# Turning z: TensorE transposes and ScalarE copies, or VectorE block transposes and SBUF-to-SBUF DMAs, with a new written order

## The chip, the cores and the metric

The kernel runs on one core of one Trainium2 chip. The metric is the device time of one execution in microseconds (us). Each time given for a kernel is a median of several runs; a profile is a record of one single execution. The engines of the core are TensorE (PE in the profile, with its weight loads as PEld), VectorE (DVE), ScalarE (ACT), GpSimd (POOL) and SyncE (SP), whose instruction queue issues most of the DMAs here.

## The reference

Two blocks follow each other. The first is a gated linear recurrence over 768 steps for 4 batches and 8 heads of width 48: a complex decay, its size held to at most 0.999, multiplies a 48x48 state, and k v is added to it; q reads it out. The second is a feed-forward block on all 3072 rows of 384 values:

```python
h = x @ w_in                       # 384 -> 1024
e = np.exp(h - h_max)
sm = e / (np.sum(e, axis=-1, keepdims=True) + 1e-09)
solu = h * sm
ln = (solu - mu) / np.sqrt(var + 1e-06) * g_ln
return (ln @ w_out).astype(np.float32)   # 1024 -> 384
```

All is float32. The kernel before and the changed one compute the same.

## The kernel before

The fast path (`whole`) cuts the 3072 rows into 24 chunks of 128 rows: chunk c has time tile c // 4 of batch c % 4. Two chunks make a group g, for which q, k, v and the two parts of the decay are loaded and prepared together (logarithms, an angle, running sums by a triangular matmul). For each chunk the prepared q and k are turned by TensorE (`f_turned`), scores are computed and masked (`f_score`, `f_att`), values and the state are multiplied in (`f_y`), and the state is carried on (`f_d`, `f_state`). Then comes the feed-forward block of that chunk (`ffn_steps`): `turn_x` and `turned_x` bring x into the layout with features on partitions; `up` multiplies by w_in into two halves of 512 columns (`f_h`, line 961); `exp` and `solu` make z, 128 rows by 1024 features (`f_z`); z is turned in two halves by four TensorE transposes each into PSUM (`f_zt`, line 981), and each half is copied to SBUF by ScalarE (`f_zT`, line 984). `down` multiplies the eight 128-row blocks of zT by w_out in two halves (`f_o`, line 1008). `norm` takes mean and variance of z by VectorE and GpSimd, `scale` multiplies the result by 1/sigma with ScalarE, `store` writes 128x384 values to DRAM.

The weights come in a wide form and are converted at the start (`fetch`, `raised`, `convert`); `again` and `inspect` load each piece of them once more later and look at its smallest value, for the check (`verdict`) that chooses between the fast path and the general one.

The order of work is written out by hand as text. Each word such as `zt0:-1` names a step and a chunk. START is gone through once; then, for n from 2 to 25, EVEN for even n and ODD for odd n, with chunk n plus the number behind the colon (`g1` means group n // 2 + 1). A step is carried out where it is first named. A step issues its instructions on the engines in this order, and each engine, SP's queue of DMAs among them, goes through its own instructions strictly in the order written, waiting where data or a buffer isn't ready. So one pair of turns, EVEN and ODD, does two chunks and one group.

Buffers that matter: `f_z` and `f_zT` have two each, `f_o` one bank of PSUM, `f_h` two banks, the PSUM pool `f_ps_t`, which all turns share, two. DMAs on SP are the loads (line 626), `load_vr` (line 637: the odd heads of v with their four 32-row blocks in reverse, eight DMAs of 32 partitions for a group), the weight pieces (line 657), the small rows `f_ends` (line 767) and `f_on` (line 826), and the stores (line 1018).

Of the kernel before, what the change touches and what calls it, by code (L numbers as in the profile page):

```python
# [11 lines left out]
FP = mybir.dt.float32  # L12
# [7 lines left out]
P = 128  # L20
# [490 lines left out]


START = """
load_ar:0 load_ai:0 fetch:0 fetch:1 fetch:4 fetch:3 clamp:0 inverse:0 fetch:2 ratio:0 raised:0 load_ar:1
tangent:0 raised:1 square:0 convert:1 secant:0 load_q:0 size:0 fourth:0 eps:0 fetch:5 convert:0 raised:4 lnm:0
load_ai:1 convert:4 total0:0 raised:2 total1:0 low0:0 raised:3 low1:0 decay:0 convert:3 qs1:0 grow:0 trig:0
angle:0 raised:5 fetch:6 qs0:0 phase0:0 convert:2 phase1:0 nearest0:0 nearest1:0 clamp:1 ends:0 part0:0 part1:0
load_k:0 raised:6 fetch:12 convert:5 ks0:0 cos:0 turn_ends:0 sin:0 exp:0 load_v:0 ks1:0 k2:0 kt1:0 tot:0 kt0:0
inverse:1 q2:0 kT1:0 gain:0 qt1:0 kT0:0 qt0:0 load_vr:0 fetch:8 q2:1 k2:1 qT1:0 convert:6 qT0:0 ratio:1 kt0:1
fetch:10 raised:12 score0:0 kt1:1 kT0:1 score1:0 qt1:1 mask0:0 fetch:9 fetch:7 fetch:11 kT1:1 load_vr:1 qt0:1  # L520
mask1:0 raised:8 qT1:1 values:0 tangent:1 score1:1 load_k:1 raised:9 mean:0 x:0 qT0:1 turn_x:0 square:1 load_q:1
convert:12 turned_x:0 secant:1 convert:8 carry:0 score0:1 size:1 raised:7 fetch:13 mask1:1 convert:7 up0:0 eps:1
raised:11 trig:1 lnm:1 angle:1 load_q:2 convert:9 raised:10 mean:1 add:0 total1:1 total0:1 mean:2 low1:1
phase0:1 low0:1 mask0:1 nearest0:1 raised:13 phase1:1 load_ar:2 convert:11 nearest1:1 fourth:1 mean:3 load_v:2
load_q:4 part0:1 part1:1 cos:1 values:1 convert:10 sin:1 x:1 convert:13 up1:0 exp:1 decay:1 qs0:1 mean:4 grow:1
mean:5 turn_x:1 q2:2 mean:6 exp0:0 mean:7 qt0:2 ks0:1 turned_x:1 k2:2 solu0:0 carry:1 centre:5 centre:2 kt0:2
kT0:2 qT0:2 up0:1 centre:7 load_ai:2 zt0:0 score0:2 centre:4 centre:3 centre:0 centre:1 exp1:0 centre:6 zT0:0
kt1:2
"""
EVEN = """  # L530
turn_x:-1 solu1:-2 score0:0 zt1:-2 down0:-2 clamp:g1 load_k:g1 inverse:g1 turned_x:-1 kt1:0 ks1:g0 zT1:-2 add:-1
again:-8 qs1:g0 kT1:0 qt1:0 ratio:g1 up0:-1 tangent:g1 q2:1 load_vr:g0 up1:-1 load_v:g0 qT1:0 square:g1 qt0:1
secant:g1 qt1:1 exp0:-1 qT0:1 k2:1 mask0:0 size:g1 score1:0 qT1:1 kt1:1 down1:-2 kt0:1 exp1:-1 norm:-2 ends:g0
kT1:1 eps:g1 kT0:1 solu1:-1 solu0:-1 mask1:0 lnm:g1 values:0 trig:g1 turn_ends:g0 tot:g0 x:0 total0:g1 low0:g1
angle:g1 scale:-2 total1:g1 score0:1 low1:g1 store:-2 zt0:-1 zT0:-1 on:g1 zt1:-1 mask0:1 score1:1 phase0:g1
zT1:-1 phase1:g1 nearest0:g1 mask1:1 carry:0 down0:-1 part0:g1 add:0 nearest1:g1 load_ai:g2 fourth:g1 part1:g1
cos:g1 again:-3 inspect:-7 turn_x:0 values:1 turned_x:0 x:1 sin:g1 up0:0 load_q:g2 up1:0 exp:g1 grow:g1 ks0:g1
k2:2 decay:g1 kt0:2 qs0:g1 exp0:0 solu0:0 q2:2 norm:-1 zt0:0 carry:1 kT0:2
"""
ODD = """  # L540
inspect:-9 qt0:1 qT0:1 zT0:-1 down1:-2 load_ar:g2 exp1:-1 scale:-2 store:-2
"""


# [8 lines left out]
def whole(ctx, tc, flag, q, k, v, a_re, a_im, moe_w_in, moe_w_out, moe_g_ln, out):  # L553
# [12 lines left out]
    nc = tc.nc  # L566
# [3 lines left out]
    FF = moe_w_in.shape[1]  # L570
# [5 lines left out]
    def pool(name, bufs, **kw):  # L576
        return ctx.enter_context(tc.tile_pool(name=name, bufs=bufs, **kw))
# [13 lines left out]
    ident, tri, _, turns, ones = (mats[:, i] for i in range(5))  # L591
# [354 lines left out]
    def ffn_steps(n):  # L946
        st = {}

        def turn_x():
            ps = st["xt"] = ps_t.tile([P, DM], FP, tag="t", padded_shape=[P, 512], name="f_xt")  # L950
            for c in range(KD):
                nc.tensor.transpose(out=ps[:, c * P:(c + 1) * P], in_=T["x", n][:, c * P:(c + 1) * P], identity=ident)  # L952

        def turned_x():
            st["xT"] = ffp.tile([P, DM], FP, tag="xT", name="f_xT")
            nc.scalar.copy(out=st["xT"], in_=st["xt"])

        def up(half):
            h = ps_h.tile([P, 512], FP, tag="h", name="f_h")
            for c in range(KD):  # L960
                nc.tensor.matmul(out=h, lhsT=st["xT"][:, c * P:(c + 1) * P],  # L961
                                 rhs=w_in[:, c, half * 512:(half + 1) * 512], start=(c == 0), stop=(c == KD - 1))
            st["h", half] = h

        def exp(half):
            if half == 0:
                st["z"] = ffp.tile([P, FF], FP, tag="z", name="f_z")
            nc.scalar.activation(out=st["z"][:, half * 512:(half + 1) * 512], in_=st["h", half], func=AF.Exp,  # L968
                                 accum_out=sums[:, n, half:half + 1])

        def solu(half):
            z = st["z"][:, half * 512:(half + 1) * 512]
            nc.vector.tensor_tensor(out=z, in0=st["h", half], in1=z, op=OP.mult)  # L973

        def turn_z(half):
            if half == 0:
                st["zT"] = zp.tile([P, FF], FP, tag="zT", name="f_zT")
            ps = st["zt", half] = ps_t.tile([P, 512], FP, tag="t", name="f_zt")
            for i in range(4):
                c = half * 4 + i  # L980
                nc.tensor.transpose(out=ps[:, i * P:(i + 1) * P], in_=st["z"][:, c * P:(c + 1) * P], identity=ident)  # L981

        def turned_z(half):
            nc.scalar.copy(out=st["zT"][:, half * 512:(half + 1) * 512], in_=st["zt", half])  # L984

        def norm():

            z = st["z"]  # L990
            bs = sml.tile([P, FF // 512, 6], FP, tag="bs", name="f_bs")
            mv = sml.tile([P, 2], FP, tag="mv", name="f_mv")
            s2 = sml.tile([P, 1], FP, tag="s2", name="f_s2")
            st["rs"] = sml.tile([P, 1], FP, tag="rs", name="f_rs")
            for i in range(FF // 512):
                nc.vector.bn_stats(out=bs[:, i], in_=z[:, i * 512:(i + 1) * 512])  # L996
            nc.vector.bn_aggr(out=mv, in_=bs)
            se = sml.tile([P, 1], FP, tag="se", name="f_se")
            nc.vector.tensor_tensor(out=se, in0=sums[:, n, 0:1], in1=sums[:, n, 1:2], op=OP.add)
            nc.vector.scalar_tensor_tensor(out=s2, in0=se, scalar=1e-6, in1=se, op0=OP.mult, op1=OP.mult)  # L1000
            nc.gpsimd.tensor_tensor(out=s2, in0=s2, in1=mv[:, 1:2], op=OP.add)
            nc.gpsimd.tensor_tensor(out=st["rs"], in0=s2, in1=mhalf, op=OP.pow)

        def down(half):
            if half == 0:
                st["o"] = ps_o.tile([P, DM], FP, tag="o", padded_shape=[P, 512], name="f_o")
            for c in range(half * KF // 2, (half + 1) * KF // 2):
                nc.tensor.matmul(out=st["o"], lhsT=st["zT"][:, c * P:(c + 1) * P], rhs=w_out[:, c],  # L1008
                                 start=(c == 0), stop=(c == KF - 1))

        def scale():
            st["out"] = ffp.tile([P, DM], FP, tag="ot", name="f_ot")
            nc.scalar.activation(out=st["out"], in_=st["o"], func=AF.Copy, scale=st["rs"])

        def store():
            ti, b = divmod(n, B)
            r0 = b * S + ti * P
            nc.sync.dma_start(out=out[r0:r0 + P, :], in_=st["out"])

        own = dict(turn_x=turn_x, turned_x=turned_x, norm=norm, scale=scale, store=store)  # L1020
        for half in range(2):
# [123 lines left out]
```

## Time and profile before

| | |
|---|---|
| median of 3 runs | 506.89 us (505.1 to 508.81) |
| profiled execution, its own time | 505.1 us |
| span of the profiled execution | 503.3 us |
| granted TensorE clock | 0.996 |
| DMA queue of SP and its share of 16 engines | 147856 packets, 43.34 MB, 38.8% |
| ScalarE copies f_zT | 48, mean 587 ns, 26.9 us |
| TensorE transposes f_zt | 192, mean 279 ns, 28.0 us |

How to read the profile: busy time is the time in which an engine has at least one instruction under way. Matmuls of TensorE overlap in the pipeline, so the mean duration of one is longer than what it costs; the distance from one start to the next is closer to that. The chain of waits is followed back from the last instruction, at each step to what released it. A window is a stretch of the span in us from its start; a timeline merges instructions of the same line that follow each other, with start, duration and count (weight loads are counted together with their matmuls, so x8 are four transposes). For a DMA, the issue is the time for which SP is held, and "to landing" the time from the issue until the data are there.

### The profile page before, as it was taken

What the parts mean: (1) busy time and instruction counts of PE and PEld (TensorE: products, weight loads), DVE (VectorE), ACT (ScalarE), POOL (GpSimd) and SP (SyncE); (2) the same over time, 40 slices, a digit from 0 to 9 for tenths busy, and PEclk for the clock granted to TensorE, in tenths of its full rate; (3) what the DMA queues carried; (4) which work ended last, traced back from release to release, by engine and by line L of the source; (5) the groups of instructions that cost most, each with busy time, mean ns of one, the idle gap of its engine ahead of it and who ended that gap; (6) DMA issues with size and microseconds to landing.
All of it is one profiled execution on the core that took longest, in us unless ns stands there. A gap on an engine that the chain in (4) does not pass through costs nothing.

```text
span 503.3 us, 15535 instructions
## 1 busy us (share of the span) xinstructions
PE 463.2 (92%) x6756; PEld 294.1 (58%) x6756; DVE 358.3 (71%) x692; ACT 314.9 (63%) x521; POOL 18.0 (4%) x52
## 2 busy tenths in 40 slices
PE   0258998999999999999999999999999999999994
PEld 0036456567566566566666666666666666667552
DVE  5899999586677687687687687687687687672331
ACT  4989948666667667657657657657657657734120
POOL 0000000000000000000000000000000000010000
PEclk9999999999999999999999999999999999999998
DMA  9867950331332542452452451452452342021001
GB/s 232 202 138 211 187 96 23 77 79 33 84 78 50 118 119 54 114 123 53 102 131 46 104 122 38 112 119 41 113 117 43 81 114 48 17 48 34 3 16 39
DMA packets 148079, 44.76 MB, mean 89 GB/s; under 512 B 141217, under 2 KB 144289, under 8 KB 148001
## 3 DMA queue, kind: packets, MB, share of 16 engines
q1 hardware_dynamic: 147856, 43.34, 38.8%
q8 instruction: 55, 0.90, 0.8%
q10 hardware_dynamic: 144, 0.33, 0.2%
q14 instruction: 24, 0.19, 0.1%
HBM read 38.87 MB, written 4.72 MB: 87 GB/s over the span
## 4 chain that ended last, share of the span: by engine, by line
PE 83%; DVE 7%; ACT 4%; DMA 2%; SPq 2%; issue 1%; ACTq 0%
PE f_o L1008 24%; PE f_h L961 23%; PE f_turned L864 8%; PE f_score L895 6%; PE f_zt L981 4%; PE f_phase L805 4%; PE f_L L754 4%; PE f_y L913 4%; PE f_d L929 3%; PE f_y L916 3%; SPq L626 2%; PE f_xt L952 1%; DMA f_raw<-in_moe_w_in_dram 1%; DMA f_v<-in_v_dram 1%; DVE f_k L854 1%
## 5 line engine op out<-in xcount | busy, mean ns | idle before, releaser
L1008 PE MATMUL f_o<-f_w_out,f_zT 128*128 128x384 f32 x384 | 132.9, 489 | 0.4 <-ACT f_zT L984 0.4
L961 PE MATMUL f_h<-f_w_in,f_xT 128*128 128x512 f32 x288 | 129.3, 597 | 0.0
L1008 PEld LDWEIGHTS f_o<-f_w_out,f_zT 128*128 128x128 f32 x384 | 69.4, 190 | 40.7 <-ACT f_zT L984 0.6
L961 PEld LDWEIGHTS f_h<-f_w_in,f_xT 128*128 128x128 f32 x288 | 52.7, 190 | 57.7 <-issue 56.4
L973 DVE TENSOR_TENSOR f_z<-f_h,f_z 128x512 f32<-128x512 f32 x48 | 32.0, 686 | 39.6 <-ACT f_z L968 39.6
L868 ACT COPY f_kT<-f_turned 96x512 f32<-96x512 f32 x48 | 27.8, 581 | 48.7 <-PE f_turned L864 48.1
L868 ACT COPY f_qT<-f_turned 96x512 f32<-96x512 f32 x48 | 26.8, 582 | 30.6 <-PE f_turned L864 30.6
L984 ACT COPY f_zT<-f_zt 128x512 f32<-128x512 f32 x48 | 26.9, 587 | 18.4 <-PE f_zt L981 18.4
L968 ACT ACTIVATE f_z<-f_h 128x512 f32<-128x512 f32 x48 | 28.6, 596 | 14.3 <-PE f_h L961 14.3
L754 PE MATMUL f_L<-f_lr,f_mats 128*128 128x384 f32 x48 | 19.9, 540 | 19.1 <-DVE f_lr L749 18.8
L895 PEld LDWEIGHTS f_score<-f_qT,f_kT 96*32 96x32 f32 x1536 | 30.6, 110 | 11.7 <-issue 11.3
L895 PE MATMUL f_score<-f_qT,f_kT 96*32 96x128 f32 (+3 forms) x1536 | 37.1, 236 | 0.0
L899 DVE TENSOR_TENSOR f_att<-f_score,f_mats 128x512 f32<-128x512 f32 x48 | 32.7, 682 | 5.8 <-PE f_score L895 5.8
L921 DVE COPY f_xn<-f_y 128x384 f32<-128x384 f32 x24 | 13.2, 552 | 30.9 <-PE f_y L916 28.4
L864 PE MATMUL f_turned<-f_mats,f_k 128*96 128x128 f32 x192 | 30.4, 283 | 5.1 <-DVE f_k L854 4.8
L864 PEld LDWEIGHTS f_turned<-f_mats,f_k 128*96 128x96 f32 x192 | 22.1, 130 | 18.9 <-issue 7.4
L996 DVE BATCH_NORM_STATS2 f_bs<-f_z 128x6 f32<-128x512 f32 x48 | 30.7, 681 | 0.0
L916 PE MATMUL f_y<-f_state,f_qT 96*32 96x48 f32 x1280 | 30.1, 205 | 0.0
L864 PE MATMUL f_turned<-f_mats,f_q 128*96 128x128 f32 x192 | 28.1, 282 | 1.9 <-ACT f_ar L732 0.8
L981 PE MATMUL f_zt<-f_mats,f_z 128*128 128x128 f32 x192 | 28.0, 279 | 0.3 <-DVE f_z L973 0.3
L916 PEld LDWEIGHTS f_y<-f_state,f_qT 96*32 96x32 f32 x1280 | 27.7, 110 | 0.0
L864 PEld LDWEIGHTS f_turned<-f_mats,f_q 128*96 128x96 f32 x192 | 21.2, 129 | 10.5 <-issue 5.4
(101 smaller groups left out, 732.7 us busy)
## 6 DMA issues: line engine op xcount, KB each, us to landing
f_raw<-in_moe_w_in_dram SPq DMA_DIRECT2D x12, 512.0 KB, 5.8
f_raw<-in_moe_w_out_dram SPq DMA_DIRECT2D x16, 384.0 KB, 4.6
f_ar<-in_a_re_dram SPq DMA_DIRECT2D x24, 192.0 KB, 3.4
f_ai<-in_a_im_dram SPq DMA_DIRECT2D x24, 192.0 KB, 4.0
f_q<-in_q_dram SPq DMA_DIRECT2D x24, 192.0 KB, 3.8
f_k<-in_k_dram SPq DMA_DIRECT2D x24, 192.0 KB, 3.7
f_v<-in_v_dram SPq DMA_DIRECT2D x24, 192.0 KB, 3.4
out_dram<-f_ot SPq DMA_DIRECT2D x24, 192.0 KB, 2.0
```

The lines of the kernel that those rows point to most:

```text
L754: nc.tensor.matmul(out=ps, lhsT=tri, rhs=st["lr"][:, i * DM:(i + 1) * DM], start=True, stop=True)
L864: nc.tensor.transpose(out=ps[0:D2, j], in_=T[nm + "2", c][:, half * 4 + j].rearrange("p u d -> p (u d)"), identity=ident)
L868: nc.scalar.copy(out=T[nm + "T", c][:, half * 512:half * 512 + 512], in_=st[nm, half][0:D2].rearrange("p i t -> p (i t)"))
L895: nc.tensor.matmul(out=ps[r0:r0 + 32, i, r:], lhsT=KT[:, x * P + r:x * P + r + 32], rhs=QT[:, x * P + r:(x + 1) * P], start=True, stop=True)
L899: nc.vector.tensor_tensor(out=st["att"][:, half * 4:half * 4 + 4].rearrange("p (i u) t -> p i u t", u=2), in0=scores[half].rearrange("p (i ...
L916: nc.tensor.matmul(out=y[r:r + 32, hs], lhsT=T["qT", c][:, x * P + r:x * P + r + 32], rhs=state[b][:, hs], start=False, stop=True)
L961: nc.tensor.matmul(out=h, lhsT=st["xT"][:, c * P:(c + 1) * P], rhs=w_in[:, c, half * 512:(half + 1) * 512], start=(c == 0), stop=(c == KD ...
L968: nc.scalar.activation(out=st["z"][:, half * 512:(half + 1) * 512], in_=st["h", half], func=AF.Exp, accum_out=sums[:, n, half:half + 1])
L973: nc.vector.tensor_tensor(out=z, in0=st["h", half], in1=z, op=OP.mult)
L981: nc.tensor.transpose(out=ps[:, i * P:(i + 1) * P], in_=st["z"][:, c * P:(c + 1) * P], identity=ident)
L996: nc.vector.bn_stats(out=bs[:, i], in_=z[:, i * 512:(i + 1) * 512])
L1008: nc.tensor.matmul(out=st["o"], lhsT=st["zT"][:, c * P:(c + 1) * P], rhs=w_out[:, c], start=(c == 0), stop=(c == KF - 1))
```

## The change

The steps `zt0`, `zt1` (TensorE) and `zT0`, `zT1` (ScalarE) fall away. In their place stand two steps for each chunk. `blocks` has VectorE transpose the whole z, 128x1024, in blocks of 32x32 into a new buffer `f_zb`, of which there is one. Each block then lies turned in its old place. `turn_z` moves the blocks to their places with 16 DMAs from SBUF to SBUF on SP's queue: for each pair of 32-partition bands r and s, one DMA takes from band r the 32 columns at s of each of the eight 128-column groups, and writes them to band s at the columns r. So each of the 16 DMAs moves 32 partitions x 8 pieces x 128 bytes, 32 KB. `down` then reads `f_zT` as before, but each of its matmuls needs all four bands. `scale` is still done by ScalarE with the same instruction; only its place in the order is new.

The three texts START, EVEN and ODD are replaced as a whole, so that every step of every engine, and every DMA, has a new place. The number of all other steps is unchanged.

```diff
--- before.py
+++ after.py
@@ -511,34 +511,34 @@
 
 
 START = """
-load_ar:0 load_ai:0 fetch:0 fetch:1 fetch:4 fetch:3 clamp:0 inverse:0 fetch:2 ratio:0 raised:0 load_ar:1
-tangent:0 raised:1 square:0 convert:1 secant:0 load_q:0 size:0 fourth:0 eps:0 fetch:5 convert:0 raised:4 lnm:0
-load_ai:1 convert:4 total0:0 raised:2 total1:0 low0:0 raised:3 low1:0 decay:0 convert:3 qs1:0 grow:0 trig:0
-angle:0 raised:5 fetch:6 qs0:0 phase0:0 convert:2 phase1:0 nearest0:0 nearest1:0 clamp:1 ends:0 part0:0 part1:0
-load_k:0 raised:6 fetch:12 convert:5 ks0:0 cos:0 turn_ends:0 sin:0 exp:0 load_v:0 ks1:0 k2:0 kt1:0 tot:0 kt0:0
-inverse:1 q2:0 kT1:0 gain:0 qt1:0 kT0:0 qt0:0 load_vr:0 fetch:8 q2:1 k2:1 qT1:0 convert:6 qT0:0 ratio:1 kt0:1
-fetch:10 raised:12 score0:0 kt1:1 kT0:1 score1:0 qt1:1 mask0:0 fetch:9 fetch:7 fetch:11 kT1:1 load_vr:1 qt0:1
-mask1:0 raised:8 qT1:1 values:0 tangent:1 score1:1 load_k:1 raised:9 mean:0 x:0 qT0:1 turn_x:0 square:1 load_q:1
-convert:12 turned_x:0 secant:1 convert:8 carry:0 score0:1 size:1 raised:7 fetch:13 mask1:1 convert:7 up0:0 eps:1
-raised:11 trig:1 lnm:1 angle:1 load_q:2 convert:9 raised:10 mean:1 add:0 total1:1 total0:1 mean:2 low1:1
-phase0:1 low0:1 mask0:1 nearest0:1 raised:13 phase1:1 load_ar:2 convert:11 nearest1:1 fourth:1 mean:3 load_v:2
-load_q:4 part0:1 part1:1 cos:1 values:1 convert:10 sin:1 x:1 convert:13 up1:0 exp:1 decay:1 qs0:1 mean:4 grow:1
-mean:5 turn_x:1 q2:2 mean:6 exp0:0 mean:7 qt0:2 ks0:1 turned_x:1 k2:2 solu0:0 carry:1 centre:5 centre:2 kt0:2
-kT0:2 qT0:2 up0:1 centre:7 load_ai:2 zt0:0 score0:2 centre:4 centre:3 centre:0 centre:1 exp1:0 centre:6 zT0:0
-kt1:2
+load_ar:0 load_ai:0 fetch:0 fetch:2 clamp:0 fetch:1 inverse:0 ratio:0 load_ar:1 fetch:6 tangent:0 raised:0
+raised:2 convert:0 fetch:4 fetch:5 square:0 secant:0 size:0 fourth:0 eps:0 load_k:0 raised:6 gain:0 convert:2
+lnm:0 total1:0 convert:6 low1:0 raised:1 fetch:3 load_q:0 total0:0 raised:4 load_ai:1 low0:0 fetch:7 decay:0
+convert:4 grow:0 trig:0 angle:0 phase0:0 raised:5 nearest0:0 phase1:0 convert:1 ks0:0 nearest1:0 fetch:9 ks1:0
+mean:0 fetch:10 convert:5 part0:0 part1:0 raised:3 cos:0 qs1:0 qs0:0 sin:0 clamp:1 q2:0 load_k:1 k2:0 k2:1 qt0:0
+exp:0 inverse:1 qT0:0 kt0:0 kt0:1 kT0:0 kT0:1 qt1:0 ratio:1 load_vr:0 score0:0 qT1:0 q2:1 tangent:1 kt1:0
+raised:7 kT1:0 square:1 secant:1 mask0:0 qt0:1 qT0:1 score1:0 convert:3 load_v:0 raised:10 mask1:0 kt1:1 kT1:1
+ends:0 qt1:1 values:0 fetch:8 qT1:1 turn_ends:0 size:1 load_q:1 score0:1 convert:7 fetch:12 x:0 eps:1 convert:10
+fetch:13 raised:8 lnm:1 raised:9 fourth:1 fetch:11 load_ai:2 load_ar:2 score1:1 trig:1 tot:0 load_vr:2 mean:1
+angle:1 convert:9 again:0 total0:1 low0:1 total1:1 mask0:1 carry:0 turn_x:0 low1:1 add:0 turned_x:0 phase0:1
+phase1:1 raised:12 convert:8 nearest0:1 mask1:1 load_v:1 mean:2 load_vr:1 nearest1:1 convert:12 mean:3 raised:13
+part0:1 mean:4 again:4 raised:11 part1:1 values:1 convert:11 up0:0 cos:1 up1:0 x:1 sin:1 exp:1 grow:1 decay:1
+clamp:2 mean:5 convert:13 ks0:1 mean:6 qs0:1 exp0:0 k2:2 inverse:2 kt0:2 solu0:0 q2:2 mean:7 exp1:0 again:2
+ratio:2 centre:4 solu1:0 turn_x:1 again:10 centre:3 blocks:0 kT0:2 turned_x:1 qt0:2 turn_z:0 tangent:2 carry:1
+kt1:2 centre:6 centre:1 qT0:2 centre:7 up1:1 qt1:2 centre:0 centre:5 kT1:2 centre:2
 """
 EVEN = """
-turn_x:-1 solu1:-2 score0:0 zt1:-2 down0:-2 clamp:g1 load_k:g1 inverse:g1 turned_x:-1 kt1:0 ks1:g0 zT1:-2 add:-1
-again:-8 qs1:g0 kT1:0 qt1:0 ratio:g1 up0:-1 tangent:g1 q2:1 load_vr:g0 up1:-1 load_v:g0 qT1:0 square:g1 qt0:1
-secant:g1 qt1:1 exp0:-1 qT0:1 k2:1 mask0:0 size:g1 score1:0 qT1:1 kt1:1 down1:-2 kt0:1 exp1:-1 norm:-2 ends:g0
-kT1:1 eps:g1 kT0:1 solu1:-1 solu0:-1 mask1:0 lnm:g1 values:0 trig:g1 turn_ends:g0 tot:g0 x:0 total0:g1 low0:g1
-angle:g1 scale:-2 total1:g1 score0:1 low1:g1 store:-2 zt0:-1 zT0:-1 on:g1 zt1:-1 mask0:1 score1:1 phase0:g1
-zT1:-1 phase1:g1 nearest0:g1 mask1:1 carry:0 down0:-1 part0:g1 add:0 nearest1:g1 load_ai:g2 fourth:g1 part1:g1
-cos:g1 again:-3 inspect:-7 turn_x:0 values:1 turned_x:0 x:1 sin:g1 up0:0 load_q:g2 up1:0 exp:g1 grow:g1 ks0:g1
-k2:2 decay:g1 kt0:2 qs0:g1 exp0:0 solu0:0 q2:2 norm:-1 zt0:0 carry:1 kT0:2
+qT1:0 score0:0 qs1:g0 tangent:g1 up0:-1 square:g1 secant:g1 ks1:g0 ends:g0 score1:0 add:-1 size:g1 load_ar:g2
+k2:1 fourth:g1 turn_ends:g0 eps:g1 mask0:0 again:4 tot:g0 up1:-1 mask1:0 lnm:g1 kt0:1 kt1:1 kT0:1 kT1:1 q2:1
+values:0 exp0:-1 total0:g1 exp1:-1 inspect:-4 qt1:1 solu0:-1 down0:-2 low0:g1 qt0:1 x:0 trig:g1 qT1:1 solu1:-1
+total1:g1 score1:1 blocks:-1 angle:g1 on:g1 low1:g1 load_q:g1 qT0:1 phase0:g1 nearest0:g1 part0:g1 load_k:g1
+phase1:g1 nearest1:g1 down1:-2 part1:g1 turn_x:0 norm:-2 turn_z:-1 norm:-1 cos:g1 turned_x:0 load_ai:g2 sin:g1
+carry:0 exp:g1 score0:1 add:0 again:-11 load_v:g1 mask1:1 up0:0 grow:g1 decay:g1 exp0:0 ks0:g1 up1:0 mask0:1
+k2:2 kt0:2 scale:-2 qs0:g1 exp1:0 kT0:2 solu0:0
 """
 ODD = """
-inspect:-9 qt0:1 qT0:1 zT0:-1 down1:-2 load_ar:g2 exp1:-1 scale:-2 store:-2
+values:0 q2:1 kt1:1 load_vr:g1 qt0:1 kT1:1 solu1:-1 down0:-2 blocks:-1 qt1:1 x:0 clamp:g2 qT0:1 inspect:-12
+inverse:g2 turn_x:0 turn_z:-1 carry:0 down1:-2 ratio:g2 turned_x:0 store:-3 scale:-2 store:-2
 """
 
 
@@ -581,6 +581,7 @@
     nat, natk = pool("f_nat", 2), pool("f_natk", 3)
     rawp, bits = pool("f_raw", 6), pool("f_bits", 3)
     xp, ffp, zp, sml = pool("f_x", 2), pool("f_ff", 2), pool("f_z", 2), pool("f_sml", 4)
+    zbp = pool("f_zb", 1)
     ps_t = pool("f_ps_t", 2, space=PSUM)
     ps_s = pool("f_ps_s", 1, space=PSUM)
     ps_y = pool("f_ps_y", 1, space=PSUM)
@@ -972,16 +973,17 @@
             z = st["z"][:, half * 512:(half + 1) * 512]
             nc.vector.tensor_tensor(out=z, in0=st["h", half], in1=z, op=OP.mult)
 
-        def turn_z(half):
-            if half == 0:
-                st["zT"] = zp.tile([P, FF], FP, tag="zT", name="f_zT")
-            ps = st["zt", half] = ps_t.tile([P, 512], FP, tag="t", name="f_zt")
-            for i in range(4):
-                c = half * 4 + i
-                nc.tensor.transpose(out=ps[:, i * P:(i + 1) * P], in_=st["z"][:, c * P:(c + 1) * P], identity=ident)
-
-        def turned_z(half):
-            nc.scalar.copy(out=st["zT"][:, half * 512:(half + 1) * 512], in_=st["zt", half])
+
+        def blocks():
+            st["zb"] = zbp.tile([P, FF], FP, tag="zb", name="f_zb")
+            nc.vector.transpose(out=st["zb"], in_=st["z"])
+
+        def turn_z():
+            st["zT"] = zp.tile([P, FF], FP, tag="zT", name="f_zT")
+            for r in range(0, P, 32):
+                for s in range(0, P, 32):
+                    nc.sync.dma_start(out=st["zT"][s:s + 32].rearrange("p (c t) -> p c t", t=P)[:, :, r:r + 32],
+                                      in_=st["zb"][r:r + 32].rearrange("p (c f) -> p c f", f=P)[:, :, s:s + 32])
 
         def norm():
 
@@ -1017,11 +1019,10 @@
             r0 = b * S + ti * P
             nc.sync.dma_start(out=out[r0:r0 + P, :], in_=st["out"])
 
-        own = dict(turn_x=turn_x, turned_x=turned_x, norm=norm, scale=scale, store=store)
+        own = dict(turn_x=turn_x, turned_x=turned_x, blocks=blocks, turn_z=turn_z, norm=norm, scale=scale, store=store)
         for half in range(2):
             own.update({f"up{half}": partial(up, half), f"exp{half}": partial(exp, half),
-                        f"solu{half}": partial(solu, half), f"zt{half}": partial(turn_z, half),
-                        f"zT{half}": partial(turned_z, half), f"down{half}": partial(down, half)})
+                        f"solu{half}": partial(solu, half), f"down{half}": partial(down, half)})
         return own
 
     def verdict():
```

## The prediction

> **What bounds the kernel now.** I read the page's shares of busy time, then the windows by stage, then the chain of waits, then the timelines of single stretches.
>
> ```profile
> PE 463.2 (92%) x6756; PEld 294.1 (58%) x6756; DVE 358.3 (71%) x692; ACT 314.9 (63%) x521; POOL 18.0 (4%) x52
> ```
> ```profile
> 0.00:20.00 20.00, 1.18 (x2) 0.84 (x3) 12.61 (x27) 12.35 (x17) 0.20 (x4) 1.00 1.03 246
> 20.00:85.00 65.00, 51.23 (x634) 30.84 (x633) 61.30 (x117) 53.42 (x83) 0.74 (x2) 1.00 0.62 131
> 100.00:440.00 340.00, 340.00 (x5336) 219.41 (x5335) 252.44 (x475) 222.45 (x369) 13.29 (x36) 1.00 0.38 84
> 240.00:278.10 38.10, 38.10 (x600) 24.58 (x600) 28.81 (x55) 24.72 (x41) 1.48 (x4) 1.00 0.42 94
> ```
> After the stretch and its length come PE, PEld, DVE, ACT and POOL busy, clock, DMA share, GB/s. There are three stages. Up to 85 us PE has gaps (85 - 52.4 = 32.6 us) and VectorE is busy for 61.3 of 65 us after the first 20. From 100 to 440 us PE has no gap at all. A pair of chunks (one EVEN and one ODD turn of the written order) repeats every 38.10 us, as the spacing of like matmuls in the chain shows. In this stage only PE work counts.
>
> ```profile
> PE f_o L1008 24%; PE f_h L961 23%; PE f_turned L864 8%; PE f_score L895 6%; PE f_zt L981 4%; PE f_phase L805 4%; PE f_L L754 4%; PE f_y L913 4%; PE f_d L929 3%; PE f_y L916 3%; SPq L626 2%; PE f_xt L952 1%; DMA f_raw<-in_moe_w_in_dram 1%; D
> ```
> The chain names f_zt, the transposes that the change takes out, with 4% of the span.
>
> ```profile
> 238.05 1.09 PE L981 MATMUL f_zt<-f_mats,f_z 128*128 128x128 f32 x8
> 239.07 0.77 PE L895 MATMUL f_score<-f_qT,f_kT 96*32 96x128 f32 x32
> ...
> 252.39 0.60 PE L981 MATMUL f_zt<-f_mats,f_z 128*128 128x128 f32 x4
> 252.92 0.88 PE L929 MATMUL f_d<-f_v,f_k 128*32 128x48 f32 x48
> ...
> 257.92 0.66 PE L981 MATMUL f_zt<-f_mats,f_z 128*128 128x128 f32 x4
> 258.41 2.75 PE L1008 MATMUL f_o<-f_w_out,f_zT 128*128 128x384 f32 x8
> ```
> Ends overlap, so cost is start to next start: 1.02 + 0.53 + 0.49 = 2.04 us a pair, 1.02 us a chunk.
>
> The new work goes to SP's queue, where the nearest thing is f_vr, 8 DMAs of 32 partitions with 128 pieces of 192 B:
>
> ```profile
> L637 SPq DMA_DIRECT2D f_vr<-in_v_dram x96: 311/430/1023, 32.8 to 450.3; - x96
> ...
> L767 SPq DMA_DIRECT2D f_ends<-f_ar x12: 512/526/608, 23.2 to 438.8; - x12
> ```
> ```profile
> SPq L637 <- DMA f_raw<-in_moe_w_out_dram: 5.1, 7, 1.3
> ```
> The first gives an issue's duration, min/median/max in ns. The second is a wait no tile explains: f_vr's buffer has nothing to do with f_raw. The last of eight f_vr issues waits for the f_raw issued before them, so it looks as if only eight DMAs are under way at once.
>
> **What the Trainium skill says.** "Vector Engine (DVE) Microarchitecture Reference", the reshape front-end section, says the 32x32 transpose sustains one element per cycle per lane; no transpose is in this trace. "Perfetto Trace Analysis", "DMA Instruction — HWDGE", says the issuing sequencer is held until the descriptors are generated, and data movement comes on top. The trace agrees: f_ends holds SP 0.526 us and lands after 1.7 us. "DMA: Bandwidth & Descriptors", "Why small descriptors are slow (HBM only)", says SBUF-to-SBUF transfers with 128-byte packets keep most of the rate; f_ends is SBUF to SBUF, but too small to test it.
>
> **The change, part by part.**
>
> PE loses 8 transposes a chunk. In the saturated stage and up to the end this is path: 23 chunks x 1.02 = **-23.5 us** (chunk 0's, at 67 to 70 us, lies where VectorE leads; I count it at nothing). The pair should fall to 38.10 - 2.04 = 36.06 us.
>
> ACT loses two copies a chunk (f_zT, 0.587 us each): 24.7 - 2.3 = 22.4 us a pair, off the path, worth nothing.
>
> VectorE gains one transpose of 128x1024 a chunk. From 384, 512 and 768 elements in 0.555, 0.686 and 0.954 us, VectorE takes 1.04 ns per element and 0.155 us; 1024 give 1.22 us, the value I take. From below 1.07 us (1024 elements at those 1.04 ns, no start); from above 2.4 us, if four-byte data take two passes. A pair goes to 28.8 + 2.4 = 31.2 us of 36.06, at worst 33.6: PE covers it; without that cover it costs the 2.4. In the opening, where VectorE leads, chunk 0's transpose counts, and chunk 1's nearly so: **+1.5 us**.
>
> SP gains 16 issues a chunk. f_vr in groups of eight takes 3.91 us (374.57) with queues light and 4.98 (260.03) behind f_raw, so 0.49 to 0.62 each. The number of pieces matters little (192 KB loads with 1024 pieces: 0.58 median). The new ones have 256 pieces; I take 0.50, bounds 0.31 (f_vr's shortest) and 0.85 (twice the median, if pieces scattered on both sides count twice). Of present work one pair shows 12.0 us (no weight reload in front of f_vr, light queues) to 16.4 us (236 to 275 us: stores 0.7, f_ai 1.1, reload 1.7 + 0.7, f_on 0.5, f_q 1.2, f_ends 0.5, f_ar 1.2, f_k 1.2, f_vr 5.0, f_v 2.5). With 14.2 in the middle: 14.2 + 32 x 0.50 = 30.2 of 36.06 us. Hidden, with 5.9 us to spare.
>
> DMA engines: while f_vr runs alone (448.5 to 450.5 us) they are 35% busy at 52 GB/s, so 0.35 x 16 x 1000 ns / 271 packets = 21 ns a packet. 4096 packets a chunk x 21 / 16 = 5.4 us, 10.8 a pair; with today's 0.42 x 38.1 = 16.0 that is 26.8 of 36. Slower than issue only above 31 ns.
>
> The new path from solu to down: transpose 1.2, 16 issues 8.0, landing about 2.1 (f_ends' 1.7 and 256 packets' 0.3), together 11.4 us with the hand-overs. In the new EVEN and ODD, the PE work written between the place of `blocks` and `down0` of that chunk is, for the even chunk: turn_x 0.45, carry 0.85, down1 2.6, two scores 1.4, up0 and up1 5.2, two turns 1.0, values 1.55, total0 0.75, one turn 0.5 = 14.3 us; for the odd chunk about the same 14.3. So **slack is about 3 us**, and the cost is nothing. What stands behind the burst on SP: in EVEN f_ai, f_on, a reload, f_v, f_ends and f_vr; in ODD the two stores, then f_ar, f_q and f_k. The stores give buffers back, and the loads are wanted 8 us or more later. `blocks` itself waits on VectorE for the earlier chunk's 16 DMAs (f_zb is one buffer); with x, add, masks queued behind it. In the written order this comes after down0, which has waited for the same DMAs, so it adds nothing. The further semaphore waits of down0 (51 ns each on PE's load queue, as f_y's are) lie under 2.6 us matmul groups.
>
> The other moved steps (weight reloads, four of them now in START and the rest in EVEN; f_ar first in EVEN; f_k and f_q early; f_vr late) keep their number of issues; I cost them at nothing in the saturated stage. In the opening the new order interleaves fetches and converts differently: zero, within 4 us either way.
>
> The end loses its cover. After the last up1, before:
>
> ```profile
> 486.87 2.74 PE L1008 MATMUL f_o<-f_w_out,f_zT 128*128 128x384 f32 x8
> 489.45 1.04 PE L981 MATMUL f_zt<-f_mats,f_z 128*128 128x128 f32 x8
> 490.90 5.43 PE L1008 MATMUL f_o<-f_w_out,f_zT 128*128 128x384 f32 x16 [0.41 <-ACT f_zT L984]
> ```
> PE idles 0.4 us there. Afterwards chunk 23 needs exp 0.8, solu 0.7, then those 11.4 us: 12.9, against down of chunk 22, 5.2 us, as the only other work. Idle 7.7; less 0.5, since landing is counted from the start of the last issue, and less the 0.4 of before: **+6.8 us**.
>
> Sum: -23.5 + 1.5 + 6.8 = -15.2. The profiled execution took 505.1 us (span 503.3 and 1.8 around it), so 489.9. That run is the fastest of three; the median, 506.9, lies 1.8 above it, and my figure for the median is **491.5 us**.
>
> **The rivals.**
> 1. *The hand-over is late.* Queues in front (f_k, f_q, a reload of 4.7 us to landing) or the eight-at-once limit push the landing 3.5 to 4 us; slack 3 is passed by 0.6 us for each of 20 chunks, or VectorE at 86% serves a mask or x late. 12 us come back: 503. For: an f_vr landing went up to 6.7 us. Against: SP waits now mostly on stores, with long idle.
> 2. *SP becomes the bound*, the case on the other side. If an issue takes 0.80 us, a pair is 14.2 + 25.6 = 39.8 us, ten pairs +17 against before, the end 6.8 + 4.8, the opening 1.5: +30, so 537. The steady stage is lost from (38.1 - 14.2)/32 = 0.75 us each; with end and opening included the sign turns at 0.72. For: the pieces are scattered on both sides, unlike any row now. Against: eight times the pieces cost f_ar only 0.15 us over f_vr.
> 3. *The VectorE transpose costs 2.4 us.* Still under PE; the opening and end lengthen by 2.4: 494.
> 4. That PE keeps the work is excluded: no transposing matmul of z is left.
>
> **How the numbers follow.** Main case 0.55 (484 to 501), rival 3 0.05, rival 1 0.17 (497 to 512), rival 2 0.23 (from 510 up). One per cent of the median, 5.1 us, is about what a measurement tells from no change. Faster: 0.55 + 0.05 + 0.03 = 0.63; within 1%: 0.11 of rival 1; slower: 0.03 + 0.23 = 0.26. The range 483 to 520 takes in rival 1 and the mild end of rival 2 and leaves out about 0.2.
>
> **What would show it.** PE without gaps from about 100 us and a period of 36.1 us; transposes near 1.22 us; the 16 issues at 0.5 us; f_o waiting for zT only in the last chunk, for about 7 us. I am wrong if PE's f_o group shows waits for DMAs in every pair, or SP has no idle time.

## The result and the profile after

The changed kernel takes **543.3 us** (median of 4 runs, 538.9 to 544.8) against 506.6 us before: the ratio is 1.071, with a 95% interval of 1.063 to 1.078. The forecast was 491.5 us with a range up to 520; the time lies outside it, on the other side. The profiled execution took 542.1 us, with a span of 540.3 us.

The page of the changed kernel first, busy time by engine and the chain of waits by engine and by line:

```profile
PE 460.4 (85%) x6564; PEld 282.2 (52%) x6564; DVE 382.0 (71%) x716; ACT 289.3 (54%) x473; POOL 18.0 (3%) x52
```
```profile
PE 38%; SPq 31%; DVE 13%; DMA 8%; ACT 4%; issue 4%; DVEq 0%; ACTq 0%
SPq L985 26%; PE f_o L1010 16%; PE f_h L962 8%; DMA f_zT<-f_zb 5%; PE f_turned L865 3%; DMA f_raw<-in_moe_w_in_dram 3%; SPq L638 3%; PE f_score L896 3%; PE f_L L755 2%; PE f_phase L806 2%; SPq L627 2%; PE f_d L930 1%; DVE f_zb L979 1%; PE f
```
The transposes are gone from TensorE, and its share fell from 92% to 85%. The chain, of which TensorE made 83% before, now has 31% of issuing on SyncE's queue; line 985, the 16 DMAs of `turn_z`, alone is 26% of the span. In the middle stage TensorE is no longer without gaps (columns as in the windows of before):

```profile
100.00:440.00 340.00, 317.22 (x4927) 197.47 (x4917) 255.56 (x465) 190.32 (x313) 11.88 (x32) 0.97 0.52 98
```
What it waits for stands in the waits (in total, times, longest):

```profile
PE f_o L1010 <- DMA f_zT<-f_zb: 38.0, 11, 8.0
...
DVE f_zb L979 <- DMA f_zT<-f_zb: 22.4, 9, 4.0
```
`down` waits for the moved blocks, and VectorE's next `blocks` waits for the same DMAs with its one buffer, with the rest of VectorE's work behind it. (The one buffer passes the delay on and does not make it: the runs below with fewer issues have the same one buffer and no such gaps. No run gave `f_zb` a second.) SyncE's timeline for one pair of chunks shows why they come late (start, duration):

```profile
246.32 11.15 SPq L985 DMA_DIRECT2D f_zT<-f_zb  x16
257.51 1.23 SPq L627 DMA_DIRECT2D f_ai<-in_a_im_dram  x2
258.83 0.58 SPq L827 DMA_DIRECT2D f_on<-f_f  x1
259.46 1.21 SPq L627 DMA_DIRECT2D f_v<-in_v_dram  x2
260.77 1.83 SPq L768 DMA_DIRECT2D f_ends<-f_ar  x1
262.65 4.78 SPq L638 DMA_DIRECT2D f_vr<-in_v_dram  x8
267.54 10.47 SPq L985 DMA_DIRECT2D f_zT<-f_zb  x16
278.11 1.75 SPq L1020 DMA_DIRECT2D out_dram<-f_ot  x2
279.96 1.15 SPq L627 DMA_DIRECT2D f_ar<-in_a_re_dram  x2
281.17 1.94 SPq L627 DMA_DIRECT2D f_q<-in_q_dram  x2
283.15 1.82 SPq L627 DMA_DIRECT2D f_k<-in_k_dram  x2
285.08 11.87 SPq L985 DMA_DIRECT2D f_zT<-f_zb  x16
```
One issue follows the other with less than 0.15 us between them. The two bursts are 21.6 us of this pair, everything else 16.3 us, and the pair lasts 38.8 us. The two new operations by themselves (durations min/median/max in ns):

```profile
L985 SPq DMA_DIRECT2D f_zT<-f_zb x384: 585/609/1958, 70.7 to 522.9; - x192
L979 DVE STREAM_TRANSPOSE f_zb<-f_z x24: 1237/1245/1247, 69.4 to 511.5; 128x1024 f32<-128x1024 f32 x24
```

**Where the 37 us are.** The starts of the first `up` matmul of chunks 2, 20 and 23 cut each kernel's span into four parts. Worked out from the traces, in us:

```
kernel            to chunk 2   2 to 20   20 to 23   23 to end   median time
before                 94.2     341.9      45.6       21.6        506.6
changed                94.3     365.5      44.4       36.1        543.3
order_alone            95.5     353.3      48.4       24.7        522.8
eight_dmas             94.6     326.2      44.4       28.6        496.4
half_on_act            99.7     377.3      49.4       29.2        562.8
odd_by_pe              96.0     346.3      46.5       28.0        519.9
half_pieces            94.2     358.8      45.7       34.6        536.8
diag_on_pool           94.9     327.1      44.6       33.3        501.3
all_on_pool            96.5     356.2      45.8       31.8        530.7
half_from_pool         93.9     345.4      45.3       36.0        521.6
loads_from_pool       104.3     340.8      45.0       37.2        531.3
contiguous_rows        95.0     349.4      46.3       34.5        531.1
last_by_pe             93.8     364.8      44.7       29.9        534.9
diag_and_last          94.4     326.9      44.5       26.1        493.5
```
The opening takes the same. Nine pairs in the middle cost 23.6 us more (40.6 in place of 38.0 us a pair), and the last chunk 14.5 us more; 20 to 23 gives 1.2 back.

### The profile page after: what moved, and what is told of

Its sections match the earlier page's. It is cut to its first block, busy times and chain, and to the rows that moved or that the text cites. A ratio compares the mean times of both kernels' runs of the same rounds, so it can differ in the third digit from the quotient of the medians.

```text
span 540.3 us, 15722 instructions
## 1 busy us (share of the span) xinstructions
PE 460.4 (85%) x6564; PEld 282.2 (52%) x6564; DVE 382.0 (71%) x716; ACT 289.3 (54%) x473; POOL 18.0 (3%) x52
## 4 chain that ended last, share of the span: by engine, by line
PE 38%; SPq 31%; DVE 13%; DMA 8%; ACT 4%; issue 4%; DVEq 0%; ACTq 0%
SPq L985 26%; PE f_o L1010 16%; PE f_h L962 8%; DMA f_zT<-f_zb 5%; PE f_turned L865 3%; DMA f_raw<-in_moe_w_in_dram 3%; SPq L638 3%; PE f_score L896 3%; PE f_L L755 2%; PE f_phase L806 2%; SPq L627 2%; PE f_d L930 1%; DVE f_zb L979 1%; PE f_y L914 1%; DVE f_w_out L693 1%
## 5 line engine op out<-in xcount | busy, mean ns | idle before, releaser
L1010 PE MATMUL f_o<-f_w_out,f_zT 128*128 128x384 f32 x384 | 147.0, 531 | 38.1 <-DMA f_zT<-f_zb 38.0
L962 PE MATMUL f_h<-f_w_in,f_xT 128*128 128x512 f32 x288 | 132.7, 604 | 0.0
L1010 PEld LDWEIGHTS f_o<-f_w_out,f_zT 128*128 128x128 f32 x384 | 76.3, 207 | 89.7 <-issue 41.9
L974 DVE TENSOR_TENSOR f_z<-f_h,f_z 128x512 f32<-128x512 f32 x48 | 32.8, 684 | 23.7 <-ACT f_z L969 23.6
L979 DVE STREAM_TRANSPOSE f_zb<-f_z 128x1024 f32<-128x1024 f32 x24 | 29.9, 1245 | 24.4 <-DMA f_zT<-f_zb 22.4
L1015 ACT ACTIVATE f_ot<-f_o,f_rs 128x384 f32<-128x384 f32 x24 | 13.9, 578 | 53.9 <-PE f_o L1010 24.2
L896 PEld LDWEIGHTS f_score<-f_qT,f_kT 96*32 96x32 f32 x1536 | 31.4, 111 | 20.8 <-issue 13.5
L755 PE MATMUL f_L<-f_lr,f_mats 128*128 128x384 f32 x48 | 22.9, 569 | 20.4 <-DVE f_lr L750 18.5
L900 DVE TENSOR_TENSOR f_att<-f_score,f_mats 128x512 f32<-128x512 f32 x48 | 32.6, 681 | 7.5 <-PE f_score L896 7.5
L758 DVE TENSOR_SCALAR f_lr<-f_L 128x384 f32<-128x384 f32 x24 | 13.4, 557 | 31.2 <-PE f_L L755 31.1
L865 PE MATMUL f_turned<-f_mats,f_q 128*96 128x128 f32 x192 | 30.4, 283 | 4.8 <-DVE f_q L855 4.0
L865 PEld LDWEIGHTS f_turned<-f_mats,f_q 128*96 128x96 f32 x192 | 23.4, 133 | 18.3 <-issue 8.4
L865 PE MATMUL f_turned<-f_mats,f_k 128*96 128x128 f32 x192 | 28.9, 283 | 3.2 <-DVE f_k L855 2.9
L865 PEld LDWEIGHTS f_turned<-f_mats,f_k 128*96 128x96 f32 x192 | 21.3, 129 | 16.6 <-issue 9.7
```

The costliest lines, as they stand in the source:

```text
L755: nc.tensor.matmul(out=ps, lhsT=tri, rhs=st["lr"][:, i * DM:(i + 1) * DM], start=True, stop=True)
L865: nc.tensor.transpose(out=ps[0:D2, j], in_=T[nm + "2", c][:, half * 4 + j].rearrange("p u d -> p (u d)"), identity=ident)
L896: nc.tensor.matmul(out=ps[r0:r0 + 32, i, r:], lhsT=KT[:, x * P + r:x * P + r + 32], rhs=QT[:, x * P + r:(x + 1) * P], start=True, stop=True)
L900: nc.vector.tensor_tensor(out=st["att"][:, half * 4:half * 4 + 4].rearrange("p (i u) t -> p i u t", u=2), in0=scores[half].rearrange("p (i ...
L979: nc.vector.transpose(out=st["zb"], in_=st["z"])
```

## The experiments

My theory after the result is rival 2 of the prediction: SyncE's queue is full, so that each new issue has to wait for the ones in front of it. Its rivals are the new order itself, the DMA engines or their bytes, and the length of one burst against its slack. All edits are to the changed kernel. Ratios are against the kernel before, on the same chip.

**The new order without the DMAs.** In place of the two steps, four transposes and a copy for each half, as before:

```diff
-            nc.vector.transpose(out=st["zb"], in_=st["z"])
...
+            for half in range(2):
+                ps = ps_t.tile([P, 512], FP, tag="t", name="f_zt")
...
+                nc.scalar.copy(out=st["zT"][:, half * 512:(half + 1) * 512], in_=ps)
```


> The new written order, but z turned by TensorE transposes and ScalarE copies as before; no block transposes and no DMAs for z. The turn of the odd chunk stands after turned_x, that of the even chunk after down0, with qT0 drawn ahead of it, because the shared PSUM buffers allow no other place. Theory (SyncE's queue is full with 16 issues a chunk): without them it has more than half of its time idle, TensorE is the bound again with 38.1 us a pair, 500 to 515 us. Rival (the new order is itself worse): 530 us or more, with TensorE gaps in the middle and SyncE idle.

Measured: 522.8 us, ratio 1.030 (1.027 to 1.033), between the two forecasts. The middle takes 39.3 us a pair. SyncE waits for 138 us on the stores alone, so it is far from full. The new order, with the turn where it had no planned place, costs 16 us; 20 us of the loss need the DMAs. The run doesn't tell how much of the 16 is the order and how much my places for the turn.

**Half the issues, the same bytes.**

```diff
-                for s in range(0, P, 32):
+                for j in range(0, P, 64):
...
-                                      in_=st["zb"][r:r + 32].rearrange("p (c f) -> p c f", f=P)[:, :, s:s + 32])
+                                      in_=st["zb"][r:r + 32].rearrange("p (c f) -> p c f", f=P)[:, :, j:j + 64])
```


> The changed kernel with 8 DMAs a chunk in place of 16: the same bytes and the same 256 pieces a DMA, but pieces of 256 bytes in place of 128. It leaves out the right placing of the blocks: the result is not z turned. Theory (issues on SyncE): a burst takes 8 x 0.65 = 5.2 us, a pair of SyncE's work 16 + 10.5 = 27 of 36 us, so TensorE is the bound and the time is 482 to 498 us. Rival (bytes or DMA engines): the landing of the last DMA is hardly earlier, 525 us or more.

Measured: 496.4 us, ratio 0.979 (0.976 to 0.982). Its middle stage, and what SyncE waits for:

```profile
100.00:440.00 340.00, 338.91 (x5367) 212.68 (x5366) 276.62 (x505) 206.29 (x341) 13.29 (x36) 1.00 0.56 108
```
```profile
SPq L985 <- DVE f_zb L979: 103.0, 20, 11.1
```
TensorE works without gaps again, at 36.2 us a pair (the forecast of the prediction was 36.06), although the DMA engines are busier than in the changed kernel (0.56 against 0.52). SyncE now waits 103 us for VectorE's blocks, where the changed kernel's SyncE waited 12.8. So neither the bytes nor the new order holds the changed kernel's middle. The run halves the issues and, with them, the pieces of a chunk (2048 in place of 4096); that it is the issues is shown together with the next two runs, which cut the pieces and keep the 16 issues.

**What an issue costs.** Two runs keep 16 issues and change what is in them. The first moves four of the eight column groups (GpSimd fills the others with ones), the second contiguous kilobytes, each from one band of partitions to the next (`to`):

```diff
-                    nc.sync.dma_start(out=st["zT"][s:s + 32].rearrange("p (c t) -> p c t", t=P)[:, :, r:r + 32],
+                    nc.sync.dma_start(out=st["zT"][s:s + 32].rearrange("p (c t) -> p c t", t=P)[:, 0:4, r:r + 32],
```


> The changed kernel with 16 DMAs a chunk of half the size: 128 pieces of 128 bytes each, for the first four column groups; the other four are filled with ones by GpSimd. It leaves out half of z's turn. If an issue is held by its pieces: near f_vr's 0.43 us with the same 128 pieces, SyncE 16.3 + 32 x 0.48 = 31.7 us a pair, TensorE bound, 490 to 508 us. If an issue of this kind costs 0.61 us whatever its size: SyncE stays full, 530 us or more.

```diff
+                    nc.sync.dma_start(out=st["zT"][to:to + 32, s:s + FF // 4], in_=st["zb"][r:r + 32, s:s + FF // 4])
```


> The changed kernel with 16 DMAs a chunk of the same 32 KB, but each one a contiguous kilobyte from each of 32 partitions: 32 pieces in place of 256. It leaves out the placing of the blocks: the result is not z turned. If an issue from SBUF to SBUF costs about 0.60 us whatever its pieces: SyncE stays full, 528 to 545 us. If the cost follows the pieces: 0.45 us or less, 490 to 508 us.

Measured: 536.8 us, ratio 1.058 (1.050 to 1.065), and 531.1 us, ratio 1.050 (1.045 to 1.055). The issues of the two runs, in this order:

```profile
L986 SPq DMA_DIRECT2D f_zT<-f_zb x384: 586/599/1838, 71.1 to 516.8; - x192
```
```profile
L986 SPq DMA_DIRECT2D f_zT<-f_zb x384: 507/589/1972, 70.1 to 510.2; - x192
```
With 256, 128 and 32 pieces the median is 609, 599 and 589 ns: these issues from SBUF to SBUF cost about 0.6 us with eight times fewer pieces or half the bytes too, while f_vr, from DRAM, still has its median of 0.43. Why the two differ is not shown by any run. Both runs stay slow, so the price goes with the issue and hardly with the piece.

**Half of the issues on other queues.** First ScalarE, then GpSimd:

```diff
-                    nc.sync.dma_start(out=st["zT"][s:s + 32]...
+                    (nc.scalar if s >= 64 else nc.sync).dma_start(out=st["zT"][s:s + 32]...
```


> The changed kernel with 8 of each 16 DMAs issued from ScalarE's queue, the other 8 from SyncE's. Theory (the issue time of one queue): both bursts take 5.2 us side by side; SyncE 27 of 36 us, ScalarE 21 + 10.4 = 31 of 36 us; 485 to 510 us, the upper end if ScalarE's waiting for z holds up the copies behind it. Rival (DMA engines or rings, shared by both queues): an issue takes twice as long in each, 530 us or more.

```diff
+                    (nc.gpsimd if s >= 64 else nc.sync).dma_start(out=st["zT"][s:s + 32]...
```


> The changed kernel with 8 of each 16 DMAs issued from GpSimd's queue, which has almost nothing else, in place of ScalarE's. If ScalarE's in-order queue was what held the run with half the issues on it at 563 us, and not the two queues' sharing of the DMA engines: SyncE 27 us a pair, TensorE bound, 488 to 510 us, unless one issue by GpSimd takes over 1.3 us. Rival (shared DMA engines or rings): 535 us or more.

Measured: 562.8 us, ratio 1.112 (1.105 to 1.119), and 521.6 us, ratio 1.027 (1.022 to 1.032). With ScalarE the issues did not slow each other down: medians 0.611 us on SyncE and 0.624 on ScalarE, so the rival that the two queues hold each other up falls too. "DMA: Bandwidth & Descriptors" of the Trainium skill, "Issuing engines are not separate DMA queues", says that a second issuing engine saves only the issuing time; here that was the scarce thing, but it was taken from an engine with other work:

```profile
ACT f_xT L957 <- DMA f_zT<-f_zb: 60.3, 11, 7.4
...
PE f_h L962 <- ACT f_xT L957: 44.6, 22, 3.8
```
ScalarE goes through its queue in order. The copy f_xT stands behind the issues and what they wait for, and TensorE's `up` waits for f_xT. The upper end of my expectation was too kind to this. With GpSimd an issue takes 0.58 us (median), SyncE waits for 115 us on VectorE's blocks, and the middle falls to 38.4 us a pair, but not to 36. There the issues stand behind norm's operations in GpSimd's queue, and the end is not better (36.0 us). I count the placing in that queue as likely, not as shown.

**GpSimd moves blocks itself.** A copy on GpSimd may go from one band of partitions to another; one run moves all 16 blocks so, one only the four on the diagonal:

```diff
+                    if r == s:        # all_on_pool: if True
+                        nc.gpsimd.tensor_copy(out=to, in_=was)
+                    else:
+                        nc.sync.dma_start(out=to, in_=was)
```


> The changed kernel with all 16 moves of 32 partitions x 256 elements as copies on GpSimd from one band of partitions to another, no DMA for z. SyncE is free as in the kernel before. The cost of such a copy is not in any run; at 0.3 to 0.9 us a chunk takes 5 to 14 us of GpSimd, a pair 10 to 29 of 36 us. Theory: TensorE is the bound, 486 to 508 us. Rival: a copy takes over 1.1 us, GpSimd becomes the bound, or norm's small operations behind the copies come late: 520 us or more.

> The changed kernel with 12 DMAs a chunk; the four blocks on the diagonal, which stay on their partitions, are copied by GpSimd, which is 3% busy. Theory (issues on SyncE): 16.3 + 24 x 0.67 = 32.4 us a pair of 36.1, TensorE bound but for the end, where a burst is 7.8 us: 497 to 510 us. Rival (a burst's length against the slack, or the new order): 520 us or more.

Measured: all 16, 530.7 us, ratio 1.045 (1.041 to 1.049), a miss. A copy has a median of 0.397 us but a mean of 0.559, and two bursts in the middle take 10.4 and 9.8 us, as long as the DMAs' did; in the even turn they stand behind norm's wait for VectorE. No run separates the two. Only the diagonal: 501.3 us, ratio 0.987 (0.982 to 0.991), as the theory had it, with 36.3 us a pair. Four issues fewer a chunk, with GpSimd doing their work, suffice.

**The loads elsewhere.**

```diff
-                    nc.sync.dma_start(
+                    nc.gpsimd.dma_start(
                         out=heads(t[:, i]), in_=src[b0 + i, :, ti * P:(ti + 1) * P, :].rearrange("h t d -> t h d")
...
-                    nc.sync.dma_start(out=vr[r:r + 32, i], ...
+                    nc.gpsimd.dma_start(out=vr[r:r + 32, i], ...
```


> The changed kernel with the 18 loads of a group (a_re, a_im, q, k, v and the eight of the reversed v) issued from GpSimd's queue; all 16 z DMAs stay on SyncE. Theory (SyncE's total, not the burst itself): SyncE 22.3 + about 5 = 27 us a pair; a burst of 10.5 with 1.25 before and 2.0 behind it is 13.8 of about 14.3 us of slack, so TensorE is the bound or nearly; 500 to 520 us, the end being as long as in the changed kernel. Rival (the burst's own length sets it, wherever the other issues are): 535 us or more. A miss upwards is also possible if norm's operations on GpSimd come late behind the loads.

Measured: 531.3 us, ratio 1.047 (1.042 to 1.052), above the expectation. Two parts are hidden in it. The middle came down by 24.7 us to 37.9 us a pair with all 16 z DMAs still in their bursts, so SyncE's total is what counts, and the burst's own length is at most 1.6 us a pair of it. GpSimd holds 0.9 us for each of the big loads:

```profile
L627 POOL DMA_DIRECT2D f_ai<-in_a_im_dram x24 | 21.5, 898 | 1.9 <-DMA f_ai<-in_a_im_dram 1.2 <-issue 0.6
```
The opening became 10 us longer. That price alone does not explain it. VectorE's first wait, for the first part of the decay, in the changed kernel and in this run:

```profile
DVE f_ar L713 <- DMA f_ar<-in_a_re_dram: 3.9, 1, 3.9
```
```profile
DVE f_ar L713 <- DMA f_ar<-in_a_re_dram: 8.9, 1, 8.9
```
The load is issued only 1.1 us later (second half at 2.3 in place of 1.2 us), but lands at 11.0 in place of 6.0 us: SyncE's queue, now free of loads, sends its weight pieces (f_raw) out at the same time, and no longer behind it. This is the likely reason, and half of the 10 us; where the rest comes from is open.

**TensorE for some chunks.** The odd chunks, and then only the last one, by TensorE and ScalarE:

```diff
         def turn_z():
             st["zT"] = zp.tile([P, FF], FP, tag="zT", name="f_zT")
+            if n % 2:         # last_by_pe: if n == NC * B - 1
+                for half in range(2):
...
+                return
```


> The changed kernel with the odd chunks' z turned by TensorE and ScalarE, at the place of turn_z; even chunks by VectorE and DMAs. Theory: SyncE has 16 + 11 = 27 us a pair, TensorE 36.1 + 1.0 = 37.1 us and is the bound; the end, where chunk 23 has no cover, is as before; 490 to 500 us, below the kernel before. Rival (new order): 525 us or more.

> The changed kernel with the z of the last chunk alone turned by TensorE and ScalarE. It measures the end by itself: from the first up of the last chunk to the end the changed kernel took 36.1 us, the one before 21.6. Theory: that difference of 14.5 us is the end's missing cover, and comes back: 526 to 532 us. Rival (the end is late because everything is): 538 us or more.

Measured: 519.9 us, ratio 1.025 (1.022 to 1.029), and 534.9 us, ratio 1.054 (1.050 to 1.058); both miss. With the odd chunks on TensorE the middle is 38.5 us a pair, where I had 37.1: TensorE waits in every pair for the first half's copy (0.68 us) and for f_xT, which comes after it on ScalarE (0.51 us). The places made for SyncE's steps are not free places for TensorE's. With the last chunk alone the end shrank from 36.1 to 29.9 us, 6.2 of the 14.5: `down` of chunk 22 still waits 2.7 us for a late burst and, after the wait, takes 7.1 in place of 5.4 us.

**Both repairs together.** 12 DMAs and the diagonal on GpSimd, and the last chunk by TensorE:

> Both repairs in one: 12 DMAs a chunk from SyncE, the four diagonal blocks copied by GpSimd, and the last chunk's z turned by TensorE and ScalarE. Theory: the run with 12 DMAs took 33.3 us from the first up of the last chunk; with 22 to 23 it comes to 487 to 494 us, 3 to 4% under the kernel before. Rival (the end is not the missing cover): 498 us or more.

Measured: **493.5 us**, ratio 0.974 (0.970 to 0.977): 13.5 us under the kernel before, about 50 under the changed one. Its middle stage and its last three groups of matmuls:

```profile
100.00:440.00 340.00, 337.76 (x5365) 212.29 (x5365) 279.01 (x504) 206.16 (x341) 53.49 (x112) 1.00 0.52 100
```
```profile
471.47 5.40 PE L1024 MATMUL f_o<-f_w_out,f_zT 128*128 128x384 f32 x16 [0.66 <-issue]
476.71 1.04 PE L990 MATMUL f_zt<-f_mats,f_z 128*128 128x128 f32 x8
478.95 5.43 PE L1024 MATMUL f_o<-f_w_out,f_zT 128*128 128x384 f32 x16 [1.21 <-ACT f_ot L1029]
```
TensorE is the bound in the middle, and the end is 4.5 us longer than before.

## Why the prediction was wrong

**The step that failed** is "SP gains 16 issues a chunk ... Hidden, with 5.9 us to spare", and in it above all the price taken for an issue, 0.50 us. The mechanism was in rival 2, with 0.23. Its sum for a pair was 14.2 + 32 x 0.50 = 30.2 us of 36.06. Between chunk 2 and chunk 20 the changed kernel's trace has 293 issues for z of 0.675 us mean, and the others come to 15.66 us a pair; from start to start 0.045 us lies between two issues (0.654 against 0.609 in a quiet burst). So z takes 32.6 x 0.72 = 23.5 and the others 15.66 + 21.4 x 0.045 = 16.6, together 40.1 of the 40.6 us a pair. The term for z was off by 7.5 us (the 0.50, taken from groups of eight f_vr, held its pauses already), the one for the others by 2.4. I had taken the price from f_vr, which reads DRAM, though two rows that I showed or counted, f_ends and f_on from SBUF to SBUF, had 0.53 and 0.51 with hardly anything in them. I argued from 1024 pieces that size matters little, which was right, and did not ask what else differs. But that better row would not have saved the forecast: 14.2 + 32 x (0.53 + 0.045) = 32.6 us still lies under 36.06, and no row of the profile before shows the 0.72 that the bursts paid. Of the prediction's own figures only rival 2's 0.80 and the upper bound of 0.85 us pass the period (39.8 and 41.4 us); "Hidden" was said of the middle value alone.

**Rival 2's own numbers** were near: 0.80 us an issue and 537 us. Its turning points, 0.75 us for the steady stage and 0.72 for the sign (0.71 by its own terms), were too high, because the other issues were held at 14.2: f_ends went from 0.53 to 1.77 us mean, f_vr from 0.42 to 0.58, f_q from 0.72 to 1.05, the stores from 0.36 to 0.50. These are means; the median of f_vr stayed at 0.43, so some issues are held for long and others not at all. A burst alone does not do it. In loads_from_pool, where the burst is whole but the loads are in another queue, the two small rows straight behind it nearly keep their price:

```profile
246.32 11.29 SPq L985 DMA_DIRECT2D f_zT<-f_zb  x16
257.70 0.58 SPq L827 DMA_DIRECT2D f_on<-f_f  x1
258.46 0.54 SPq L768 DMA_DIRECT2D f_ends<-f_ar  x1
```
There f_ends takes at most 0.63 us, in the changed kernel, with loads between the burst and it, up to 3.3. What in the queue does it is open.

**The DMA engines** were right to be left out, and overpriced: 21 ns a packet, where the queue's share and packets, after less before, give (0.520 x 540.3 - 0.388 x 503.3) x 16 / 104448 = 13 ns. At 128 bytes in 13 ns, 16 engines kept busy would move some 158 GB/s, an estimate, against 246 in the first 20 us of the kernel before; the "most of the rate" that the prediction cites for such packets is about two thirds here. The eight-at-once limit that I read out of f_vr's wait did no harm in the bursts, where a DMA lands 2.0 us after its issue and eight issues take 5.2; and it does not explain the held issues, since f_ends at 260.77 us was held for 1.83 us with four DMAs under way.

**VectorE** was right: 1.245 us against 1.22, a price worked out from other operations at 1.04 ns an element. So a turned element costs what theirs do, which agrees with the one element per cycle of the Trainium skill's "Vector Engine (DVE) Microarchitecture Reference", the reshape front-end section, if theirs take a cycle too; no run shows the cycle itself. The pair's VectorE work is hidden as soon as SyncE is not the bound.

**TensorE's gain** was right where the queue allows it: 36.2 and 36.3 us a pair in the two runs with fewer issues.

**The opening**, forecast at +1.5, was +0.1. **The end**, forecast at +6.8, was mis-sized twice. From the last `up` to the last `down` I had 12.4 us, and it took 15.7 with a burst of 10.7 in place of 8.0. And the last `down` did not take 5.2 us:

```profile
511.50 5.40 PE L1010 MATMUL f_o<-f_w_out,f_zT 128*128 128x384 f32 x16 [2.34 <-DMA f_zT<-f_zb]
524.90 8.32 PE L1010 MATMUL f_o<-f_w_out,f_zT 128*128 128x384 f32 x16 [8.00 <-DMA f_zT<-f_zb]
```
After 8 us without work the same matmuls take 8.3 us. The windows of the two groups, the second cut in two, show the granted clock (the third number from the end):

```profile
511.50:516.90 5.40, 5.40 (x16) 2.92 (x16) 4.37 (x11) 0.00 (x0) 1.20 (x4) 1.00 0.29 73
524.90:530.50 5.60, 5.60 (x9) 3.16 (x10) 1.61 (x11) 0.00 (x0) 0.00 (x0) 0.50 0.33 101
530.50:533.30 2.80, 2.80 (x10) 1.24 (x8) 0.00 (x0) 0.00 (x0) 0.00 (x0) 0.95 0.00 0
```
Half the clock for 5.6 us costs 2.8 us, nearly all of the difference. I had priced waits of TensorE at their length alone. With the two, 6.8 + 3.3 + 3.1 = 13.2 us, against 14.5 less the 1.2 that the stretch before it gives back.

**Rival 1**, the late hand-over, had slack of about 3 us; loads_from_pool, with full bursts and a free SyncE, puts its cost at no more than 1.6 us a pair.

## What to carry to other kernels

An added burst of DMAs is priced first by its number of issues on the queue that issues them, with the price of the nearest row of the same kind (SBUF to SBUF here) as the lower bound and a good deal more as the upper one (here 0.53 before, 0.675 in the burst), with the pause between issues, and with what the issues already there take, which can rise too; bytes and DMA engines come after that. If that sum is near the period, fewer issues is the repair: here moving four blocks of 16 to GpSimd turned a loss of 7% into a gain of 1.3%, while half of the issues on ScalarE's queue made it worse, and on GpSimd's left it slower than the kernel before. At the end of this kernel, where TensorE has no other work to cover a wait, the wait also cost half of its clock for a while, so the last chunk deserves a form of its own.

## What the runs showed of the hardware

In medians, an issue on SyncE from SBUF to SBUF holds the queue for 0.59 to 0.61 us with 32, 128 or 256 pieces (16 or 32 KB), 0.51 to 0.53 for the rows of 3 KB in the kernel before, against 0.43 from DRAM for 24 KB (f_vr) and 0.36 to DRAM (stores, in quiet). The same issue takes 0.62 us from ScalarE and 0.58 from GpSimd; a load of 192 KB takes 0.89 us from GpSimd, 0.58 from SyncE. GpSimd copies 32x256 float32 values from one band of partitions to the same or another in 0.39 us (median), and more when it goes on for 16 (mean 0.56). And TensorE's matmuls of 128x384, 5.4 us for 16 with their loads in a busy stage, took 8.3 us after 8 us of waiting, with a granted clock of 0.50 for the first 5.6 us; the mean granted clock of the changed kernel was 0.950 against 0.996.
